# Products on a tile of ones at the head of a fused attention and soft-MoE kernel, and VectorE's fills of memory moved in front

## The chip, the cores and the metric

The kernel runs on 1 core of one Trainium2 chip. The metric is the device time of one execution in microseconds (us). TensorE (PE) multiplies, VectorE (DVE), ScalarE (ACT) and GpSimd (POOL) do the rest; GpSimd's queue issues all loads (with a conversion from float32 to bf16 on the way), SyncE's queue the stores.

## What is computed

Two stages follow each other. Attention with a softmax that has one extra term in its sum, over q, k and v of shape (8, 12, 448, 64), so 96 heads:

```python
scores = scale * np.matmul(q, k.transpose(0, 1, 3, 2))
m = np.max(scores, axis=-1, keepdims=True)
e = np.exp(scores - m)
attn = e / (np.sum(e, axis=-1, keepdims=True) + np.exp(-m) + 1e-09)
attn_out = np.matmul(attn, v)
```

Its result, turned into x of shape (3584, 768), goes through a mixture of experts with soft slots (8 experts, 4 slots each, hidden size 1024):

```python
logits = x @ phi
d = softmax(logits, over the 3584 rows);  c = softmax(logits, over the 32 slots)
slot_input = d.T @ x
slot_out[e] = np.maximum(slot_input[e] @ w1[e], 0.0) @ w2[e]
out = c @ slot_out
```

## The kernel before, in words

The order on every engine is the order of the program text; there is no scheduler. The 96 heads are worked in 48 pairs n, three pairs to a group g of loads. For a pair the steps are:

- `load(g, nm)` (L154 to L168): loads q, k or v of a group from GpSimd's queue. For group 0, q and k come pair by pair (`pl`), so six small loads, then v in two, then q and k of group 1. `make_identity` runs on GpSimd after the first two loads.
- `T(n)` (L214, product L224): 28 transposes of 64x64 on TensorE, two at a time on the two halves of the rows, into one buffer of `psA`; a copy to `R` follows, on ScalarE (L227) or VectorE (L229).
- `A(n, i)` (L237): scores with the queries on the partitions, for quarter i of the 448 queries. Quarters 0 to 2 are two products of 448 columns (L246), one for each head of the pair, each in a buffer of `psA`, and a row maximum on VectorE for each (L250); quarter 3 is two products in one buffer (L256) and one maximum (L259). So a pair costs VectorE seven maxima. `As(c)` runs the next c quarters in the list of all. Later in the kernel `A1` (L261, product L268, maximum L270) does the same for one head.
- `W1(g)`, `W2(g)`, `W3(g)`: GpSimd negates the maxima (L277), TensorE turns them (L297, and L298 with `ident2`), ScalarE takes them to `mT` (L303).
- `Bk(n, i)` (L313): scores with the keys on the partitions (L332, L335; later L354, L358 in `AB`), buffers of `psB`, and ScalarE's exponential into the five buffers of `e2`.
- `V(g)` (L372): GpSimd copies v into `vp`, whose columns of ones VectorE has written.
- `AV(n, i, qs)` (L381, product L393): the exponentials times v, in the one bank of `psV`. `N1` and `N2` divide, `PX` turns the result, and `P(b)` does logits and the sums over slots after each of the 8 batches.

`psA` has three buffers, so a product of `A` waits until the maximum three buffers back has been read. The experts follow after the last pair (`hidden`, `turn`, `slots`, `out_mm` at L793), and the stores.

At the start, ahead of the first pair, VectorE forms `ident2` and `identf` from `ident` (L181, L182), then fills memory: `halfm` (L190, L192), the two tiles `wm` (L194), the two tiles `vp` with their columns of ones (L196 to L199) and `ones` (L200, L201). After that come the first steps of the pipeline, written out by hand:

```python
T(0)
As(2)
T(1)
As(2)
W1(0)
V(0)
load(1, "v")
As(1)
T(2)
W2(0)
```

Then a loop over the pairs, of two half steps each, runs `As`, `Bk`, `T`, `AV` and the rest; its first five half steps run three quarters of `A` between `Bk`'s products and one at the end.

Of the kernel before, what the change touches and what calls it, by code (L numbers as in the profile page):

```python
# [8 lines left out]
F32 = mybir.dt.float32  # L9
# [15 lines left out]
HG = 6  # L25
NP = 3
W65 = 65
# [4 lines left out]
def kernel(  # L32
# [10 lines left out]
    nc = tc.nc  # L43
    B, H, S, D = q.shape
# [27 lines left out]
    ones = const.tile([128, 2], BF16, name="ones")  # L72
    sel = const.tile([128, HG], BF16, name="sel")
    phi_sb = const.tile([128, KC, NS], BF16, name="phi_sb")
    halfm = const.tile([128, 2], F32, name="halfm")
# [13 lines left out]
    part = lambda nm, o, z: R[:, at_[nm] + o:at_[nm] + o + z]  # L89
# [3 lines left out]
    vp = [part(f"vp{i}", 0, VPN).rearrange("p (h i d) -> p h i d", h=HG, i=4) for i in range(2)]  # L93
    wm = [part(f"wm{i}", 0, 512).rearrange("p (i c) -> p i c", i=4) for i in range(2)]
# [48 lines left out]
    with ExitStack() as at:  # L143
# [5 lines left out]
        psV = pool("psV", 1, space=PSUM)  # L149
# [4 lines left out]
        def load(g, nm, l0=0, l1=NP):  # L154


            b, h0 = g // 2, (g % 2) * HG
            src = {"q": q, "k": k, "v": v}[nm][b, h0:h0 + HG]
            if nm != "v":
                t = part(f"nq{g % 2}", "qk".index(nm) * NP * S, NP * S).rearrange("p (l x) -> p l x", l=NP)  # L160
                x = src.rearrange("(l h) (j t) d -> (h j) l (t d)", h=2, t=7)
                gdma(out=t[:, l0:l1, :], in_=x[:, l0:l1, :])
            else:
                t = part("nv", 0, NATV).rearrange("p (h t d) -> p h t d", h=HG, t=4)
                x = src.rearrange("h (p t) d -> p h t d", t=7)
                gdma(out=t[0:64], in_=x[:, :, 0:4, :])
                gdma(out=t[64:128], in_=x[:, :, 3:7, :])
            nat[nm, g] = t  # L168

        for pl in range(NP):  # L170
            load(0, "q", pl, pl + 1)
            load(0, "k", pl, pl + 1)
            if pl == 0:
                make_identity(nc, ident)
# [9 lines left out]
        for base in (0, 64):  # L184
# [2 lines left out]
                out=sel[base:base + 64], in_=sel[base:base + 64], fill=1.0,  # L187
                compare_op=ALU.not_equal, base=0,
                pattern=[[-1, HG]], channel_multiplier=1)
        nc.vector.memset(halfm, 0.0)  # L190
        for hl in range(2):
            nc.vector.memset(halfm[64 - 64 * hl:128 - 64 * hl, hl:hl + 1], 1.0)  # L192
        for t in wm:
            nc.vector.memset(t, 0.0)  # L194
        for t in vp:
            nc.vector.memset(t, 0.0)  # L196
            nc.vector.memset(t[:, :, 0:3, D:W65], 1.0)
            nc.vector.memset(t[0:64, 0:HG:2, 3, D:W65], 1.0)
            nc.vector.memset(t[64:128, 1:HG:2, 3, D:W65], 1.0)  # L199
        nc.vector.memset(ones, 1.0)  # L200
        nc.vector.memset(ones[64:128, 1:2], 0.0)  # L201
        gdma(out=phi_sb, in_=moe_phi.rearrange("(j p) s -> p j s", p=128))

        mx, ngm, ec, mT, eT, av, us = {}, {}, {}, {}, {}, {}, {}
# [9 lines left out]
        def T(n):  # L214
            g, pl = divmod(n, NP)
            ps = psA.tile([128, 2, S], BF16, tag="a", name="ps_t")
            for a in range(2):
                src = nat["qk"[a], g]
                for tok in range(7):
                    for hl in range(2):  # L220

                        c = kcol(hl, tok) if a else (2 * tok if tok < 4 else 2 * tok - 7) * 64
                        r = slice(64 * hl, 64 * hl + 64)
                        nc.tensor.transpose(ps[r, a, c:c + 64], src[r, pl, tok * D:(tok + 1) * D], ident[r, r])  # L224
            t = qk_t[n % NQK]
            if n < 6 or pl == 0:
                nc.scalar.copy(t, ps)  # L227
            else:
                nc.vector.tensor_copy(t, ps)  # L229
            qkT[n] = t  # L230
# [6 lines left out]
        def A(n, i):  # L237
            g, pl = mg(n), n % NP
            if pl == mpl(g)[0] and i == 0:
                mx[g] = psm.tile([128, 21], F32, tag="mx", name="mx")  # L240
            t = qkT[n]
            if i < 3:
                pss = [psA.tile([128, 512], F32, tag="a", name="ps_a") for _ in range(2)]
                for hl in range(2):
                    r = slice(64 * hl, 64 * hl + 64)
                    nc.tensor.matmul(pss[hl][:, 0:S], t[r, 0, i * 128:(i + 1) * 128], t[r, 1, :],  # L246
                                     start=True, stop=True)
                for hl in range(2):
                    c = HG * i + 2 * pl + hl
                    nc.vector.reduce_max(mx[g][:, c:c + 1], pss[hl][:, 0:S], axis=AX.X)  # L250
            else:
                ps = psA.tile([128, 512], F32, tag="a", name="ps_a")

                for hl in range(2):
                    r = slice(64 * hl, 64 * hl + 64)
                    nc.tensor.matmul(ps[64 - 64 * hl:128 - 64 * hl, 0:S], t[r, 0, 384:448], t[r, 1, :],  # L256
                                     start=True, stop=True)
                c = 3 * HG + pl
                nc.vector.reduce_max(mx[g][:, c:c + 1], ps[:, 0:S], axis=AX.X)  # L259
# [13 lines left out]
        def W1(g):  # L273
            w, m = wm[g % 2], mx[g]
            l0, l1 = mpl(g)
            nm = psm.tile([128, 21], BF16, tag="ngm", name="ngm")
            neg = lambda o, s: nc.gpsimd.tensor_scalar(o, s, -1.0, None, op0=ALU.mult)  # L277
            cols = lambda t: t[:, 0:3 * HG].rearrange("p (i c) -> p i c", i=3)[:, :, 2 * l0:2 * l1]
            o = w[:, 0:3, :].rearrange("p i (d c) -> p i d c", d=2)[:, :, :, 2 * l0:2 * l1]
            neg(o, cols(m).unsqueeze(2).to_broadcast([128, 3, 2, 2 * (l1 - l0)]))  # L280
            for hl in range(2):
                r = slice(64 - 64 * hl, 128 - 64 * hl)
                o = w[r, 3, :].rearrange("p (d c) -> p d c", d=2)[:, :, 2 * l0 + hl:2 * l1:2]
                neg(o, m[r, 3 * HG + l0:3 * HG + l1].unsqueeze(1).to_broadcast([64, 2, l1 - l0]))
            if l1 - l0 == NP:
                neg(nm, m)
            else:
                nc.gpsimd.memset(nm, 0.0)
                neg(cols(nm), cols(m))
                neg(nm[:, 3 * HG + l0:3 * HG + l1], m[:, 3 * HG + l0:3 * HG + l1])  # L290
            ngm[g] = nm
# [313 lines left out]
        def As(c):  # L605
            for _ in range(min(c, len(runs))):
                A(*runs.pop(0))


        T(0)  # L610
        As(2)
        T(1)
        As(2)
        W1(0)
        V(0)
        load(1, "v")
# [102 lines left out]
        n = NPAIR - 1  # L719
# [107 lines left out]
        for half in range(2):  # L827
            ps = psA.tile([128, 512], F32, tag="a", name="ps_cs")
            r = slice(64 * half, 64 * half + 64)
            for b2 in range(2):  # L830
                nc.tensor.matmul(ps[64 * b2:64 * b2 + 64, 0:2 * B], identf[r, r], crec[r, b2::2, :],
                                 start=True, stop=True)
# [54 lines left out]
```

## Time and profile before

| | us |
|---|---|
| median of 3 runs | 310.43 (310.2 to 311.73) |
| profiled execution, its own time | 310.7 |
| its span, first to last instruction | 308.9 |

| engine | busy us | share of the span |
|---|---|---|
| PE | 275.6 | 89% |
| DVE | 257.2 | 83% |
| ACT | 249.3 | 81% |
| POOL | 202.7 | 66% |

The page cuts the span into 40 slices of 7.7 us and gives busy tenths of each engine. A line of the timeline gives the start in us, the busy time, engine, line of the kernel, operation, output and input, shapes, the number of instructions merged, and in brackets the idle time of the engine before it with what ended it. The chain of waits follows the work that ended last back from the end. "PEld" is TensorE's load of weights, beside its products. Durations of products are modelled from their start and include the way through the array, so two that follow each other overlap.

### The profile page before, as it was taken

To read this page: it belongs to the slowest core of one execution; us is meant where nothing else is said; L and a number is where in the kernel's file an instruction comes from. 1 tells how busy PE (TensorE), PEld (TensorE's weight loads), DVE (VectorE), ACT (ScalarE), POOL (GpSimd) and SP (SyncE) were. 2 spreads that over 40 slices of the span, in tenths; PEclk is the share of its full clock that TensorE was granted. 3 is DMA by queue.
4 is the path that set the end of the run, shared out by engine and by line. 5 is a ranking of instruction groups with operands and counts; after the bars stand their busy time and mean duration, and the time that the engine had idled before them with its cause. 6 is when DMAs were issued, how large, how long until landed. Compare 5 with 4: busy or idle time off the path is not lost.

```text
span 308.9 us, 12205 instructions
## 1 busy us (share of the span) xinstructions
PE 275.6 (89%) x5067; PEld 159.0 (51%) x5068; DVE 257.2 (83%) x607; ACT 249.3 (81%) x549; POOL 202.7 (66%) x403
## 2 busy tenths in 40 slices
PE   2899999999999999999999999999999899994810
PEld 1434456565666656665566566656665556451200
DVE  4778999999999999999999999999999566536930
ACT  2357599999999999999999999999999997236810
POOL 8682769788788878896889788879584863000000
PEclk9999999999999999999999999999999999999555
DMA  6999499999999999999999999999971999937997
GB/s 88 149 128 202 64 205 150 198 182 205 163 196 157 210 169 198 155 203 149 149 164 186 177 186 169 196 177 203 166 110 17 144 126 204 337 128 260 415 439 312
DMA packets 49350, 57.44 MB, mean 186 GB/s; under 512 B 2832, under 2 KB 41488, under 8 KB 48912
## 3 DMA queue, kind: packets, MB, share of 16 engines
q0 software_dynamic: 45536, 42.52, 90.1%
q1 hardware_dynamic: 3760, 14.16, 11.5%
q8 instruction: 39, 0.64, 0.8%
q14 instruction: 15, 0.12, 0.1%
HBM read 88.18 MB, written 14.16 MB: 331 GB/s over the span
## 4 chain that ended last, share of the span: by engine, by line
PE 50%; DVE 30%; ACT 7%; issue 4%; POOL 4%; DMA 1%; DVEq 0%; POOLq 0%
DVE mx L270 15%; PE ps_av L393 11%; PE ps_a L268 6%; PE ps_t L224 6%; PE ps_b L354 5%; PE ps_b L358 4%; DVE mx L250 3%; DVE mx L259 3%; PE ps_b L332 3%; PE ps_a L246 2%; DVE W L801 2%; DVE R L229 2%; PE ps_x L445 2%; ACT R L227 2%; PE ps_so L764 2%
## 5 line engine op out<-in xcount | busy, mean ns | idle before, releaser
L270 DVE TENSOR_REDUCE mx<-ps_a 128x1 f32<-128x448 f32 x248 | 136.6, 613 | 5.3 <-PE ps_a L268 5.1
L360 ACT ACTIVATE R<-ps_b 128x448 bf16<-128x448 f32 x272 | 131.0, 573 | 1.1 <-PE ps_b L358 0.8
L268 PE MATMUL ps_a<-R 64*128 64x448 bf16 x248 | 80.5, 352 | 1.8 <-DVE mx L270 1.8
L354 PE MATMUL ps_b<-R 64*128 64x448 bf16 x272 | 73.9, 353 | 0.9
L358 PE MATMUL ps_b<-mT,sel 64*128 64x448 bf16 x272 | 70.6, 350 | 0.0
L393 PEld LDWEIGHTS <-R 128*128 128x128 bf16 (+1 forms) x1536 | 50.5, 101 | 30.5 <-issue 26.4
L393 PE MATMUL ps_av<-R 128*128 128x65 bf16 (+1 forms) x1536 | 64.9, 196 | 0.1
L419 POOL TENSOR_TENSOR R<-ubuf,rec 128x384 bf16<-128x384 f32 x44 | 36.3, 825 | 37.9 <-DVE rec L415 23.4
L224 PEld LDWEIGHTS <-R 64*64 64x64 bf16 x1344 | 31.1, 113 | 19.2 <-issue 7.8
L338 ACT ACTIVATE R<-ps_b 128x448 bf16<-128x448 f32 x64 | 36.0, 579 | 5.9 <-PE ps_b L335 5.9
L224 PE MATMUL ps_t<-ident,R 64*64 64x64 bf16 x1344 | 32.0, 198 | 5.9 <-DMA R<-in_q_dram 4.3
L451 ACT CAST R<-ps_x 128x512 bf16<-128x512 f32 x47 | 28.1, 598 | 5.7 <-PE ps_x L445 5.7
L259 DVE TENSOR_REDUCE mx<-ps_a 128x1 f32<-128x448 f32 x48 | 29.6, 616 | 0.6 <-PE ps_a L256 0.3
L358 PEld LDWEIGHTS <-sel 64*128 64x128 bf16 x272 | 21.5, 94 | 14.9 <-issue 5.3
L268 PEld LDWEIGHTS <-R 64*128 64x128 bf16 x248 | 23.1, 94 | 9.8
L405 ACT COPY ubuf<-ps_av 128x455 f32<-128x455 f32 x44 | 25.2, 573 | 3.0 <-PE ps_av L393 2.8
L227 ACT COPY R<-ps_t 128x896 bf16<-128x896 bf16 x20 | 18.4, 922 | 11.3 <-PE ps_t L224 11.0
L250 DVE TENSOR_REDUCE mx<-ps_a 128x1 f32<-128x448 f32 x40 | 22.6, 618 | 4.3 <-PE ps_a L246 3.9
L332 PE MATMUL ps_b<-R 64*64 64x448 bf16 (+1 forms) x112 | 22.7, 386 | 0.0
L335 PE MATMUL ps_b<-mT,sel 64*64 64x448 bf16 (+1 forms) x112 | 21.5, 366 | 0.0
L424 POOL TENSOR_TENSOR R<-ubuf,rec 128x128 bf16<-128x128 f32 x44 | 17.5, 398 | 3.7
L354 PEld LDWEIGHTS <-R 64*128 64x128 bf16 x272 | 17.2, 94 | 4.7 <-issue 0.2
(132 smaller groups left out, 454.0 us busy)
## 6 DMA issues: line engine op xcount, KB each, us to landing
W<-in_moe_w_dram POOLq DMA_DIRECT2D x22, 768.0 KB, 9.5
R<-in_v_dram POOLq DMA_DIRECT2D x32, 192.0 KB, 4.6
out_dram<-W SPq DMA_DIRECT2D x2, 2688.0 KB, 10.3
R<-in_q_dram POOLq DMA_DIRECT2D x15, 336.0 KB, 7.4
R<-in_k_dram POOLq DMA_DIRECT2D x15, 336.0 KB, 8.5
wd<-in_moe_w_dram POOLq DMA_DIRECT2D x8, 384.0 KB, 10.0
R<-wd SPq DMA_DIRECT2D x8, 384.0 KB, 8.6
R<-in_moe_w_dram POOLq DMA_DIRECT2D x2, 768.0 KB, 8.3
```

The lines of the kernel that those rows point to most:

```text
L224: nc.tensor.transpose(ps[r, a, c:c + 64], src[r, pl, tok * D:(tok + 1) * D], ident[r, r])
L250: nc.vector.reduce_max(mx[g][:, c:c + 1], pss[hl][:, 0:S], axis=AX.X)
L259: nc.vector.reduce_max(mx[g][:, c:c + 1], ps[:, 0:S], axis=AX.X)
L268: nc.tensor.matmul(ps[:, 0:S], t[r, 0, i * 128:(i + 1) * 128], t[r, 1, :], start=True, stop=True)
L270: nc.vector.reduce_max(mx[g][:, c:c + 1], ps[:, 0:S], axis=AX.X)
L332: nc.tensor.matmul(outs[hl], t[rs[hl], 1, cols], t[rs[hl], 0, :], start=True, stop=False)
L338: nc.scalar.activation(e, p[:, 0:S], AF.Exp, scale=scale)
L354: nc.tensor.matmul(ps[hl][:, 0:S], t[rs[hl], 1, cols], t[rs[hl], 0, :], start=True, stop=False)
L358: nc.tensor.matmul(ps[hl][:, 0:S], sel[rs[hl], h:h + 1].to_broadcast([64, 128]), mT[mg(n)][rs[hl], :], start=False, stop=True)
L360: nc.scalar.activation(e[:, hl, :], ps[hl][:, 0:S], AF.Exp, scale=scale)
L393: nc.tensor.matmul(o, eT[n, i, hl][:, qc], vp[g % 2][:, 2 * pl + hl, i, 0:W65], start=(i == 0 and u == 0 and hl == 0), stop=(i == 3), skip ...
L419: eng.tensor_mul(x[:, 0:3, c:c + 128].rearrange("p i (h d) -> p i h d", h=2), u[:, 0:6, 0:D].rearrange("p (i h) d -> p i h d", h=2), rec[: ...
```

## The change

A view `warm_t` of the first 512 columns of `e2` is filled with ones by VectorE as its first instruction, followed by all its fills of `halfm`, `wm`, `vp` and `ones`. TensorE gets seven products of 512 columns on that tile, with 128x128 of it as weights, ahead of everything else; they write a tile of the `psV` pool that nothing reads. The loads, `make_identity`, `ident2`, `identf` and `sel` follow in the text. GpSimd's order of instructions is as before. Five more such products, of 448 columns, stand between the first steps: two after T(0), one inside the first `As(2)`, one inside the second and one after it.

```diff
-        for pl in range(NP):
-            load(0, "q", pl, pl + 1)
-            load(0, "k", pl, pl + 1)
-            if pl == 0:
-                make_identity(nc, ident)
-        load(0, "v")
-        load(1, "q")
-        load(1, "k")
-
-
-        for h in range(2):
-            nc.vector.tensor_add(ident2[:, 64 * h:64 * h + 64], ident[:, 0:64], ident[:, 64:128])
-        nc.vector.tensor_copy(identf, ident)
-        nc.gpsimd.memset(sel, 0.0)
...
+        warm_t = part("e2", 0, 512)
+        nc.vector.memset(warm_t, 1.0)
+        ps_w = psV.tile([128, 512], F32, tag="v", name="ps_warm")
+
+        def warm(n, cols=512):
+            for _ in range(n):
+                nc.tensor.matmul(ps_w[:, 0:cols], warm_t[:, 0:128], warm_t[:, 0:cols], start=True, stop=True)
+
         nc.vector.memset(halfm, 0.0)
...
         nc.vector.memset(ones, 1.0)
         nc.vector.memset(ones[64:128, 1:2], 0.0)
+        warm(7)
+        for pl in range(NP):
+            load(0, "q", pl, pl + 1)
+            load(0, "k", pl, pl + 1)
+            if pl == 0:
+                make_identity(nc, ident)
...
         T(0)
-        As(2)
+        warm(2, S)
+        As(1)
+        warm(1, S)
+        As(1)
         T(1)
-        As(2)
+        As(1)
+        warm(1, S)
+        As(1)
+        warm(1, S)
         W1(0)
         V(0)
```

More of the change, by code (lines that the diff above doesn't have):

```diff
@@ L168, in load @@
             nat[nm, g] = t
+        warm_t = part("e2", 0, 512)
[4 more added lines that the diff above has]
+                nc.tensor.matmul(ps_w[:, 0:cols], warm_t[:, 0:128], warm_t[:, 0:cols], start=True, stop=True)
+        nc.vector.memset(halfm, 0.0)
+        for hl in range(2):
+            nc.vector.memset(halfm[64 - 64 * hl:128 - 64 * hl, hl:hl + 1], 1.0)
+        for t in wm:
+            nc.vector.memset(t, 0.0)
+        for t in vp:
+            nc.vector.memset(t, 0.0)
+            nc.vector.memset(t[:, :, 0:3, D:W65], 1.0)
+            nc.vector.memset(t[0:64, 0:HG:2, 3, D:W65], 1.0)
+            nc.vector.memset(t[64:128, 1:HG:2, 3, D:W65], 1.0)
+        nc.vector.memset(ones, 1.0)
+        nc.vector.memset(ones[64:128, 1:2], 0.0)
+        warm(7)
         for pl in range(NP):
@@ L189 @@
                 pattern=[[-1, HG]], channel_multiplier=1)
[L190 to L201, printed above, removed]
         gdma(out=phi_sb, in_=moe_phi.rearrange("(j p) s -> p j s", p=128))
```

## The prediction, made before the changed kernel ran

> **What bounds it.** I read the page first, then the timeline of the first 40 us, the chain of waits there, and a table of stretches cut at one repeated event.
>
> ```profile
> PE 275.6 (89%) x5067; PEld 159.0 (51%) x5068; DVE 257.2 (83%) x607; ACT 249.3 (81%) x549; POOL 202.7 (66%) x403
> DVE  4778999999999999999999999999999566536930
> PEclk9999999999999999999999999999999999999555
> ```
>
> VectorE is at 9 tenths from the fifth slice on, but has holes in the first four (31 us). The clock row says "full" there; the durations disagree. From the timeline:
>
> ```profile
> 8.27 0.95 PE L224 MATMUL ps_t<-ident,R 64*64 64x64 bf16 x28
> 22.97 0.82 PE L393 MATMUL ps_av<-R 128*128 128x65 bf16 x12
> 23.73 0.36 PE L246 MATMUL ps_a<-R 64*128 64x448 bf16 x2
> 31.41 0.63 PE L224 MATMUL ps_t<-ident,R 64*64 64x64 bf16 x28 [0.18 <-DVE mx L259]
> 31.97 0.54 PE L393 MATMUL ps_av<-R 128*128 128x65 bf16 x12
> ```
>
> The same 28 transposes take 0.95 us early and 0.63 later, the same 12 products 0.82 and 0.54; an L246 pair takes 0.55 to 0.58 before 23 us and 0.36 at 23.73. So TensorE runs at about half clock until some 23.5 us; the clock row simply has no record before that. What this costs is read from VectorE's waits:
>
> ```profile
> 7.06 2.22 DVE L250 TENSOR_REDUCE mx<-ps_a 128x1 f32<-128x448 f32 x4
> 9.74 1.16 DVE L250 TENSOR_REDUCE mx<-ps_a 128x1 f32<-128x448 f32 x2 [0.47 <-PE ps_a L246]
> 11.04 0.62 DVE L259 TENSOR_REDUCE mx<-ps_a 128x1 f32<-128x448 f32 x1
> 13.68 2.22 DVE L250 TENSOR_REDUCE mx<-ps_a 128x1 f32<-128x448 f32 x4 [0.95 <-PE ps_a L246]
> ```
>
> and from stretches cut where the maxima of A(1,1), A(2,1), A(3,1) and so on begin: equal work, seven maxima each.
>
> ```profile
> 13.68:18.79 5.11, 4.94 (x44) 1.80 (x44) 4.00 (x7) 3.02 (x8) 5.05 (x9) 1.00 0.79 85
> 18.79:24.12 5.33, 5.01 (x59) 2.30 (x58) 4.09 (x7) 2.80 (x5) 4.04 (x11) 1.00 1.16 156
> 24.12:28.60 4.48, 4.18 (x69) 2.14 (x69) 3.81 (x7) 3.67 (x9) 1.07 (x3) 1.00 1.32 205
> 28.60:32.83 4.23, 3.57 (x56) 1.65 (x56) 4.09 (x9) 2.51 (x5) 0.00 (x0) 1.00 0.90 138
> 32.83:37.31 4.48, 3.96 (x66) 2.04 (x67) 4.34 (x8) 2.37 (x6) 4.33 (x7) 1.00 0.26 25
> ```
>
> Columns: length, then busy time of PE, PEld, DVE, ACT, POOL. Two steps at half clock last 5.11 and 5.33 us with TensorE nearly full (4.94, 5.01); three at full clock last 4.48, 4.23 and 4.48, mean 4.40, with VectorE nearly full. The start is bound by TensorE at half clock, what follows by VectorE and TensorE together.
>
> **The change, part by part.** The sum is against the profiled execution: span 308.9, time 310.7, so 1.8 lie outside; it is 0.27 above the median of 310.43.
>
> *Fills moved.* VectorE's fills (L190 to L201) ran from 3.56 to 7.03; its first maximum began at 7.06, but that maximum's product ended only at 6.46 + 0.55 = 7.01. Moved in front, where VectorE sat idle 3.1 us for `ident`, fills plus the 0.6 of `ident2` and `identf` (L181, L182) end near 0.75 + 0.5 + 3.5 + 0.6 = 5.35. Alone that gains 0.03; with a faster product the maximum is free to start earlier. `ident2` and `identf` are not read before L298 at 12.89, so their delay costs nothing. SP's queue has nothing here, POOL's order is unchanged: the same issues, from 1.25 on.
>
> *Seven products in front.* The new fill is 512 bf16 elements of value 1; L196 takes 0.72 for 792 elements, so about 0.5. VectorE can start at 0.75, as ScalarE does (its table load), so the products can start near 1.3. A 448-column step at half clock is 0.37 (chain of waits, L332); 512 columns are 0.42, seven 2.94, ending near 4.25. The first transpose waits for q until 4.35, so q's transfer hides them with 0.1 to spare. Bounds: 0 if that holds, 0.3 late if the fill starts late; I take 0. No row shows an all-ones fill this early; L196 is nearest.
>
> *Five products in the waits*, 0.37 each at half clock, 0.19 at full. Two after T(0): TensorE idles from 5.5 to 6.46 for ScalarE's copy; hidden. One inside As(2): the next product's maximum queues behind two others until 8.17; hidden. One after A(0,2): the hole before 10.42 is 0.6; hidden. The last delays A(1,0) from 10.93 to 11.17 at half clock, up to 0.24; at full clock nothing. I charge 0.1. They write the bank that AV(0) takes at 22.97, long after.
>
> *What full clock brings*, if it comes by about 6.5 us:
> - First maximum: its product takes 0.36, not 0.55: 0.20.
> - A(0,2): T(1) starts with a freed bank near 8.07 and takes 0.63 plus 0.36, to 9.06; VectorE is busy until 9.08. The hole of 0.47 closes.
> - A(0,3): product 0.37, not 0.58; the hole of 0.14 before 11.04 closes.
> - A(1,1): hole 0.95. Before it POOL turns the maxima (L277) until 12.34, which no clock shortens; L297 starts 0.2 earlier, its step shrinks by 0.2, the product by 0.19: 0.6.
> - The two steps of 5.11 and 5.33 become 4.40: 0.71 + 0.93 = 1.64.
>
> Sum 0.20 + 0.47 + 0.14 + 0.6 + 1.64 = 3.05, less 0.1: about 2.9. The ceiling is all VectorE idle time from 7.06 to 24.13, 17.07 - 13.16 = 3.9. Next late is VectorE's own row of maxima. The gain should carry to the end: in the table of waits TensorE waits for a transfer once only, the 4.3 at the start, and POOL issues later loads in program order, earlier with the rest.
>
> *Does the clock come?* Unbroken TensorE work from 14.36 to 18.77 (4.41 us in the chain) did not raise it; from 20.03 to about 23.7 did. Most products there use half the array, paired. Seven full-array products back to back are denser than either, though only 2.94 long; then come 0.9 of transposes and 0.75 of products. I take it that it rises between 4.5 and 6.6. It must also stay: 28.60 to 32.83 held full clock with PE busy 3.57 of 4.23, and the new start is at least about as busy.
> The Trainium skill, TensorE: Matmul & The Clock Gate, Part 1, asks for about 3.4 us of sustained work in a free-running window; by it the seven alone fall short in some phases and the two after T(0) must help. Its Part 4 says that transposes do not count as busy; by that rule the gap grows and the forecast leans to the first rival's 310.7. No run here shows a start with dense products.
>
> *The tail.* At the end the clock halves near 286. Products of L793 on the chain after 289 sum to 3.1 us. A shifted start can move that drop against the work: at most 1.5 gained, 0.5 lost; I take 0.
>
> 310.7 - 2.9 = 307.8, and I forecast 307.8 for the median as well.
>
> **The rivals.**
> *The clock stays low or falls back.* For it: 4.41 us of unbroken work did not raise it. Against: the density above. Then the five products cost up to 0.24, and the time is 310.5 to 310.9, say 310.7; a rise one step late (near 13.7) keeps the 1.64 alone, about 309.1. Chance 0.15.
> *The gain is given back later*, by POOL or a transfer that becomes the bound. For it: the software queue's packets fill 90.1% of the span. Against: the single transfer wait, and q of group 2, issued at 16.25 with a median of 7.4 to landing, is used at 31.4. Time 309 to 310.4. Chance 0.07.
> *Slower: VectorE's fills hold back POOL's issues.* Fills now run beside the first q and k issues and the making of `ident`. If each held POOL until they end near 4.8, q would land up to 3.55 later than 4.30, TensorE would idle between the seven products and T(0), lose the clock, and the time be 310.7 + 3.5 = 314.2. It decides from a delay of 2.9 if the clock stays, of 1.6 (0.5%, about what a measurement here can tell) if it is lost. Against:
>
> ```profile
> 1.95 0.55 POOL L162 DMA_DIRECT2D R<-in_k_dram  x1
> 3.59 0.54 POOL L162 DMA_DIRECT2D R<-in_k_dram  x1
> 4.63 0.56 POOL L162 DMA_DIRECT2D R<-in_k_dram  x1
> ```
>
> The second and third lay beside fills, the first beside an idle VectorE: no difference. Chance 0.08.
> The Trainium skill, SBUF - State Buffer, SBUF: two separate sides, describes this trap (VectorE locking POOL out while it writes descriptors), which would give the 314.2; its Who interferes with whom exempts instructions with at most one input in SBUF, as fills are, which gives 307.8. The rows side with the exemption.
>
> **How the numbers follow.** Forecast 0.70, rivals 0.15, 0.07, 0.08. Faster by over 0.5% means below 308.9: the forecast. Within: both gentle rivals, 0.22. Slower: 0.08. The range goes down to 306.5 (the ceiling of 3.9, 306.8, and some of the tail) and up to 310.6, into the first rival; outside lie the slow rival and a few hundredths on each side.
>
> **What would show it.** Right: transposes of T(1) at 0.63, not 0.95; L246 pairs near 0.36 from 6.5 us; the hole of 0.47 gone, that of 0.95 down to about 0.35; steps near 4.4 from the first; the maxima of A(3,1) about 2.9 earlier than 24.12, and the last store earlier by the same. Wrong: half-clock durations past 10 us; a first transpose later than 4.5; q issues longer than 0.7; or A(3,1) early but the end not.

## The result, and the profile after

The changed kernel took 308.6 us (median of 11 runs, 307.47 to 310.6) against 311.27 for the kernel before (median of 11, 309.84 to 312.0): ratio 0.9922, 95% interval 0.99 to 0.9943, or 2.4 us. Twice more, beside the experiments, the ratio was 0.9881 (0.9839 to 0.9923) and 0.9938 (0.99 to 0.9977). The forecast was 307.8, against a median of 310.43 that stands at 311.27 now that there are more runs.

The first profile of the changed kernel is of an execution of 310.6 us, the slowest of its runs, with a span of 308.8 against 308.9 before. It is the more instructive for that: it shows the gain made and then lost. In this kernel's numbering L224 of before is L233, L246 is L255, L250 is L259, L539 is L548. From the page, busy tenths and clock:

```profile
PE   7878999999999999989999999999999899994810
DVE  5969999999999999979999999999999566536930
PEclk9979999999999999999999999999999999999555
```

VectorE fills its second and fourth slice as before it did only from the fifth, but has new holes in slices 3 and 18, and the clock row shows a 7 in slice 3, where before it had no record at all. The start, from the timeline:

```profile
0.93 0.48 DVE L171 MEMSET R<- 128x512 bf16 x1 [0.93 <-PEq L886]
1.47 3.17 PE L176 MATMUL ps_warm<-R 128*128 128x512 bf16 x7 [1.47 <-DVE halfm L178]
4.57 0.85 PE L233 MATMUL ps_t<-ident,R 64*64 64x64 bf16 x28
5.46 0.91 ACT L236 COPY R<-ps_t 128x896 bf16<-128x896 bf16 x1 [3.43 <-PE ps_t L233]
6.82 3.32 DVE L259 TENSOR_REDUCE mx<-ps_a 128x1 f32<-128x448 f32 x6 [1.54 <-PE ps_a L255]
8.03 0.63 PE L233 MATMUL ps_t<-ident,R 64*64 64x64 bf16 x28 [0.19 <-DVE mx L259]
12.02 2.22 DVE L259 TENSOR_REDUCE mx<-ps_a 128x1 f32<-128x448 f32 x4 [0.20 <-PE ps_a L255]
```

T(1) takes 0.63 us, which before was first so for T(4), at 26.9 us; six maxima follow each other without a hole where there was one of 0.47; the hole before A(1,1) is 0.20, not 0.95, and A(1,1) starts at 12.02, not 13.68. In the trace's record of the clock, full speed begins at 5.15 us (23.64 before). Then:

```profile
14.82 0.41 PE L233 MATMUL ps_t<-ident,R 64*64 64x64 bf16 x14 [0.18 <-DVE mx L268]
16.66 0.41 PE L233 MATMUL ps_t<-ident,R 64*64 64x64 bf16 x14 [1.43 <-DMA R<-in_k_dram]
17.40 2.22 DVE L259 TENSOR_REDUCE mx<-ps_a 128x1 f32<-128x448 f32 x4 [1.57 <-PE ps_a L255]
20.20 0.95 PE L233 MATMUL ps_t<-ident,R 64*64 64x64 bf16 x28
25.22 0.63 PE L233 MATMUL ps_t<-ident,R 64*64 64x64 bf16 x28 [0.18 <-DVE mx L268]
```

T(3) does its 14 transposes of q, then stands 1.43 us for k of group 1. Soon after, the clock falls, and T(4) at 20.20 takes 0.95 again. The stretches between 5.2 and 30 us (columns as above; the sixth number after the length is the granted clock):

```profile
5.20:18.80 13.60, 10.01 (x145) 4.33 (x141) 10.29 (x20) 6.20 (x11) 12.03 (x26) 1.00 1.16 146
18.81:22.20 3.39, 3.39 (x51) 1.90 (x50) 2.50 (x5) 2.36 (x4) 3.05 (x9) 0.50 1.17 171
22.30:30.00 7.70, 6.75 (x103) 3.13 (x103) 6.92 (x13) 5.43 (x12) 1.24 (x3) 1.00 1.30 202
```

So the lead over the kernel before was 2.7 us at A(2,0), 14.7 us in, and 1.7 at A(3,1) (22.42 against 24.12). It stayed 1.7 to 1.8 up to 131 us, and was lost there:

```profile
131.48 0.25 PE L233 MATMUL ps_t<-ident,R 64*64 64x64 bf16 x5 [0.34 <-issue]
138.50 0.18 PE L548 MATMUL ps_s<-cd,R 128*128 128x32 bf16 x1 [1.28 <-issue]
```

TensorE stops after 23 of 28 transposes, and again after 23 of 28 products, for 0.34 and 1.28 us, with no wait that the profile shows. From 139 us on the lead is 0.1. The profile of the kernel before has no such stop.

### The profile page after: what moved, and what is told of

The parts are those of the page before. It is cut to its first block, busy times and chain, and to the rows that moved or that the text cites. A ratio compares the mean times of both kernels' runs of the same rounds, so it can differ in the third digit from the quotient of the medians.

```text
span 308.8 us, 12231 instructions
## 1 busy us (share of the span) xinstructions
PE 276.0 (89%) x5079; PEld 159.0 (51%) x5080; DVE 257.2 (83%) x608; ACT 249.4 (81%) x549; POOL 203.4 (66%) x403
## 4 chain that ended last, share of the span: by engine, by line
PE 49%; DVE 27%; ACT 7%; POOL 5%; issue 4%; DMA 3%; DVEq 0%; POOLq 0%
DVE mx L279 14%; PE ps_av L402 11%; PE ps_a L277 6%; PE ps_b L363 5%; PE ps_t L233 5%; PE ps_b L367 4%; DMA R<-in_k_dram 3%; DVE mx L259 3%; PE ps_b L341 3%; DVE mx L268 2%; PE ps_x L454 2%; PE ps_so L779 2%; PE ps_o L808 2%; PE ps_h L763 2%; DVE R L238 2%
## 5 line engine op out<-in xcount | busy, mean ns | idle before, releaser
L233 PEld LDWEIGHTS <-R 64*64 64x64 bf16 x1344 | 30.3, 110 | 16.5 <-issue 7.1
L233 PE MATMUL ps_t<-ident,R 64*64 64x64 bf16 x1344 | 31.0, 195 | 3.6 <-DMA R<-in_k_dram 1.4
L259 DVE TENSOR_REDUCE mx<-ps_a 128x1 f32<-128x448 f32 x40 | 22.5, 618 | 5.3 <-PE ps_a L255 5.1
L341 PE MATMUL ps_b<-R 64*64 64x448 bf16 (+1 forms) x112 | 21.8, 374 | 0.0
L344 PE MATMUL ps_b<-mT,sel 64*64 64x448 bf16 (+1 forms) x112 | 20.7, 353 | 0.0
```

What stands on the lines that cost most here:

```text
L341: nc.tensor.matmul(outs[hl], t[rs[hl], 1, cols], t[rs[hl], 0, :], start=True, stop=False)
```

## The experiments

The theory now: the seven products raise the clock, the five hold it, and two things can take a part back, k's transfer and TensorE's stops. Rivals: the moved fills carry the gain; the five alone do; any busy TensorE does, whatever share of the array works; the stops belong to the change. In each list below, "lead" is against the profiled execution of the kernel before, at the first maximum of A(3,1) (24.12 us there) and at the last store's issue.

**again**: the changed kernel, unchanged.

> The changed kernel once more, for a second profile. In its first profile the lead over the kernel before was 2.7 us at 14.7 us, 1.7 from 22 us on, and 0.1 from 139 us on, after TensorE had stood 0.3 us at 131.1 and 1.3 us at 137.2 with nothing to wait for. Theory 'chance': those two stops are not of the change, so this profile keeps a lead of 1.7 to 2.7 us to the end and its span is 306 to 307.2. Rival 'given back': the shifted program meets them each time, and the lead is gone at 139 us again, span 308.5 or more. Timed, either way, 0.990 to 0.994 of the kernel before.

Median 307.4 (6 runs); before 311.39 (29 runs); ratio 0.9881 (0.9839 to 0.9923). Clock up at 5.42 us, T(3) waits for k (landed at 17.02), clock down at 19.08 for 3.4 us; lead 1.4 at A(3,1) and 1.2 at the last store. No stop at 131 to 139. The ratio is better than the 0.990 to 0.994 expected. The lead kept to the end is a little under what "chance" expected; the span of 307.4 lies between the two forecasts. The stops are not part of each execution. The wait for k is:

```profile
17.06 0.41 PE L233 MATMUL ps_t<-ident,R 64*64 64x64 bf16 x14 [1.69 <-DMA R<-in_k_dram]
```

**fills_only**: fills in front, no products.

```diff
-        warm_t = part("e2", 0, 512)
-        nc.vector.memset(warm_t, 1.0)
...
-        warm(7)
...
-        warm(2, S)
...
```

> VectorE's fills in front, none of the twelve products. Theory 'clock': the transposes of T(1) still take 0.95 us, the first maximum starts within 0.1 us of 7.06, the ratio is 0.999 to 1.001. Rival 'order': the moved fills carry the gain, and the ratio is 0.990 to 0.994 as for the whole change.

Median 310.89 (12 runs), ratio 0.9982 (0.9945 to 1.0018). The first maximum starts at 7.03, not 7.06, T(1) takes 0.96, clock up at 23.41 (23.64 before); the lead at A(4,1) is 0.1. The moved fills alone bring nothing that the runs can show; the interval does not hold the 0.9922 of the whole change.

**seven_only** and **seven_look**: the same kernel twice, without the five.

```diff
-        warm(2, S)
-        As(1)
-        warm(1, S)
-        As(1)
+        As(2)
...
-        warm(1, S)
-        As(1)
-        warm(1, S)
+        As(1)
```

> The seven products in front, none of the five in the waits. Theory 'the seven raise the clock, the five only guard it': in most runs the whole gain, ratio 0.990 to 0.995; in the profile full clock by about 7 us. Rival 'the five are needed': the clock stays at half or falls back before 14 us, ratio 0.997 to 1.000.

> The seven without the five once more, one look. In the first the clock rose at 23.6 us only. Theory 'the seven can raise it, in some positions of a clock of its own, and the five hold it': full clock by 5.5 us and back to half before 15 us, or as in the first look. Rival 'the seven never raise it': half clock to 17 us or later again.

seven_only: median 310.92 (12 runs), ratio 0.9986 (0.9954 to 1.0019), no gain to be seen; its profile had half clock to 23.64 us. seven_look is one execution, of 310.48 us, and its profile caught the clock in the act (transposes of T(0), T(1), T(2), then stretches of the same run):

```profile
4.57 0.95 PE L233 MATMUL ps_t<-ident,R 64*64 64x64 bf16 x28
8.14 0.63 PE L233 MATMUL ps_t<-ident,R 64*64 64x64 bf16 x28 [0.19 <-DVE mx L259]
11.07 0.96 PE L233 MATMUL ps_t<-ident,R 64*64 64x64 bf16 x28 [0.23 <-DVE mx L268]
```

```profile
6.00:9.40 3.40, 2.02 (x34) 0.83 (x34) 2.47 (x5) 1.07 (x2) 3.18 (x7) 1.00 1.12 146
9.50:23.00 13.50, 12.53 (x137) 5.65 (x136) 10.53 (x19) 6.66 (x14) 10.69 (x26) 0.50 1.18 154
```

Half, full, half: up at 6.0 us, down at 9.4, up at 23.1. The seven can raise the clock, and without the five it fell back 3.4 us later, though TensorE was busy 2.02 of 3.40 us. The timed runs say how often. Time ahead of the first record counts as full clock in a run's mean granted clock (0.964 in the profile of the kernel before, despite its start), so a rise without a fall leaves no mark in it, but a fall does: it is 0.941 in seven_look, and 0.938 to 0.945 in 7 of the 12 runs of seven_only, against 0.961 to 0.964 in the other five, of which one is the profile with half clock to 23.64. So the seven alone raised the clock in at least 7 of 12 runs, and there it fell back. In fills_only, five_only and half_rows no run is under 0.958.

**five_only**: without the seven.

```diff
-        warm(7)
```

> The five products in the waits, not the seven in front. Theory 'the seven raise the clock': full clock comes somewhat earlier than in the kernel before, between 10 and 17 us, for the waits are denser: a third to two thirds of the gain, ratio 0.994 to 0.998. Rival 'the five do it': T(1) at 0.63 us and ratio 0.990 to 0.994. Rival 'density in the waits does nothing': half clock past 17 us, ratio 0.999 to 1.001.

Median 310.19 (12 runs), ratio 0.9965 (0.9935 to 0.9996). Clock up at 18.07 us; lead 1.3 at A(3,1). The ratio is the theory's; the clock, in the one profile, rose later than its 10 to 17 us, as in the last rival. The rise came 5.6 us earlier than before (23.64), so the five can bring it forward; what that is worth, some 1.1 us by the ratio, has an interval of 0.1 to 2.0.

**half_rows**: all twelve on 64 rows of the array.

```diff
-                nc.tensor.matmul(ps_w[:, 0:cols], warm_t[:, 0:128], warm_t[:, 0:cols], start=True, stop=True)
+                nc.tensor.matmul(ps_w[:, 0:cols], warm_t[0:64, 0:128], warm_t[0:64, 0:cols], start=True, stop=True)
```

> The twelve products with 64 rows of the tile instead of 128: the same number of columns and the same time each, half of the array at work. Theory 'the share of the array counts': the clock does not rise in front, the products only fill time, ratio 0.996 to 1.000, half clock past 13 us. Rival 'only time counts': as the change, full clock by about 7 us in most runs, ratio 0.988 to 0.994.

Median 310.93 (12 runs), ratio 0.999 (0.9959 to 1.0021). The seven take the same time, but the clock stays at half to 23.45:

```profile
1.47 3.17 PE L176 MATMUL ps_warm<-R 64*128 64x512 bf16 x7 [1.47 <-DVE halfm L178]
8.32 0.95 PE L233 MATMUL ps_t<-ident,R 64*64 64x64 bf16 x28
11.84 0.96 PE L233 MATMUL ps_t<-ident,R 64*64 64x64 bf16 x28
```

Time alone does not count, the share of the array does. The profile alone would not show it, for in seven_only's profile the full array did not raise the clock either; the 12 runs do, with an interval that does not hold 0.9922 and no granted clock under 0.959.

**split_next**: the first third of group 1's q and k ahead of the rest.

```diff
-        load(1, "q")
-        load(1, "k")
+        load(1, "q", 0, 1)
+        load(1, "k", 0, 1)
+        load(1, "q", 1, NP)
+        load(1, "k", 1, NP)
```

> The changed kernel with the first third of the next group's q and k (all that T(3) reads) loaded ahead of their other two thirds, so two more issues on GpSimd's queue. In both profiles of the change T(3) stood 1.4 to 1.6 us for k of group 1, and the clock then fell for 3.4 us at about 19 us. Theory 'the transfer takes back a part': k's third lands before 15 us, the wait is gone, the clock stays up past 19 us, and the maximum of A(3,1), at 22.4 in the first profile of the change, starts near 20.8; 1 to 1.7 us faster than the changed kernel, ratio to before 0.983 to 0.989. Rival 'another wait takes its place': v or GpSimd's later start of W1 holds, and the ratio is that of the change, 0.989 to 0.993.

Median 308.16 (6 runs), ratio 0.9891 (0.9855 to 0.9926). k's third landed at 12.65, T(3) did not wait (1.43 and 1.69 us in the two profiles of the change), A(1,1) to A(2,1) took 3.77 us (5.38 in the first profile of the change). But in this profile the clock had already fallen, from 9.42 to 12.83:

```profile
6.10:9.40 3.30, 2.58 (x36) 1.00 (x35) 2.48 (x5) 0.97 (x2) 3.23 (x7) 1.00 1.17 143
9.50:12.80 3.30, 3.30 (x39) 1.58 (x38) 2.52 (x5) 0.57 (x2) 2.56 (x9) 0.50 1.25 183
```

Even so the lead was 2.9 at A(3,1) and 2.7 at the last store, with a span of 306.2. A(3,1) began at 21.20, not near 20.8. The transfer's part is confirmed in the profile; the ratio is the rival's, so in the medians the kernel is not told from the change.

**hold**: four more products ahead of T(3).

```diff
+                if hs == 0:
+                    warm(4, S)
                 if hs < 5:
                     T(hs + 3)
```

> The changed kernel with four more products of 448 columns ahead of T(3), in the time in which TensorE waits for k of group 1. The transfer is not moved. Theory 'the wait costs twice, by itself and by the clock': the wait of 1.4 to 1.6 us stays, but full clock holds past 19 us, and A(3,1) starts 0.5 to 0.9 us earlier than 22.4; ratio to the kernel before 0.986 to 0.990. Rival 'the fall of the clock does not matter there': the same ratio as the change, 0.989 to 0.993.

Median 308.01 (6 runs), ratio 0.9886 (0.9849 to 0.9924). The clock rose at 4.47 and held to 284; lead 3.3 at A(3,1), then two stops at 85 and 98 us, and 1.5 at the last store. As a test of the wait it is inconclusive: this time k landed at 15.19, and T(3) began at 15.63, after the four products. Whether it would have waited without them is not shown.

**dense** and **again2**: split_next with four more products, beside the change on the same chip. The diff leaves out the load order. (The text on dense says that T(3) waited for k in hold; that was misread: it stood behind the four products.)

```diff
         T(0)
         warm(2, S)
         As(1)
-        warm(1, S)
+        warm(2, S)
         As(1)
         T(1)
         As(1)
-        warm(1, S)
+        warm(2, S)
...
+                if hs == 0:
+                    warm(2, S)
                 if hs < 5:
                     T(hs + 3)
```

> The load order of split_next, and four more products: two instead of one inside each As(2), two ahead of T(3). In split_next the clock fell at 9.4 us with the waits of 6.0 to 9.4 filled by one product, and the lead was 2.7 us; in hold it never fell, but T(3) still waited 0.9 us for k, and the lead was 3.3. Theory 'clock and transfer are two separate losses': neither comes, the lead over the kernel before at A(6,1) is 3.5 to 4.3 us, and the ratio to the kernel before is 0.984 to 0.988. Rival 'the start is by then bound by VectorE': the lead is 3.3 or less, ratio 0.988 to 0.991, as hold and split_next.

> The changed kernel beside dense on the same chip. Ratio to the kernel before 0.988 to 0.994; dense is 0.5 to 1.5 us faster by its median if the lead of its start counts, within 0.4 us if TensorE's stops at random places cover it.

dense: median 308.23 (8 runs, 307.4 to 308.39), ratio 0.9907 (0.9873 to 0.9941). Clock up at 5.64, held to 282; lead 3.6 at A(3,1), 3.5 at A(6,1), 2.2 at the last store, after one stop of 1.1 at 188 us. The lead is the theory's at its lower end, the ratio the rival's. again2: median 308.5 (9 runs, 307.39 to 311.65), ratio 0.9938 (0.99 to 0.9977), and the best start of all, lead 4.0 at A(3,1): this time k landed at 15.14, and T(3) hardly waited:

```profile
14.70 0.89 PE L233 MATMUL ps_t<-ident,R 64*64 64x64 bf16 x28 [0.18 <-DVE mx L268]
15.92 2.22 DVE L259 TENSOR_REDUCE mx<-ps_a 128x1 f32<-128x448 f32 x4 [0.21 <-PE ps_a L255]
18.72 0.63 PE L233 MATMUL ps_t<-ident,R 64*64 64x64 bf16 x28 [0.18 <-DVE mx L268]
```

By 177 us half of that lead was gone, most of it in these two stops, and 1.8 was left at the last store:

```profile
129.61 0.25 PE L233 MATMUL ps_t<-ident,R 64*64 64x64 bf16 x5 [0.54 <-issue]
176.12 0.43 PE L402 MATMUL ps_av<-R 128*128 128x65 bf16 x9 [0.98 <-issue]
```

dense is 0.3 us faster by its median, within the 0.4 of "stops cover it". Its runs lie closer together, but with 8 against 9 runs and the same fastest time (307.4), no version here is shown to beat the change. The two slowest runs of again2, 310.36 and 311.65 us, have a mean granted clock of 0.948 and 0.939 (0.958 to 0.963 in its other seven): there the clock fell back in the changed kernel too, 0.939 being as low as in seven_look. No run of dense is under 0.96. With two runs against none, that the extra products prevent the fall is not shown.

## Why the prediction was right, and where it was not

- **Half clock at the start, and its price.** Right. The starts with full clock and no late transfer bear the mechanism out; the sizes were too small. In again2 A(1,1) started 1.78 earlier (1.41 in the sum: 0.20 + 0.47 + 0.14 + 0.6), and the two next steps took 4.02 and 4.23 us, not 4.40: 2.2 instead of 1.64. Together 3.97 instead of 3.05. The most mis-sized term is the step: three later ones were averaged, though the first step of the start has no products of AV yet and the second has 12, as the later step of 4.23. The rest is mostly the first maximum, 0.36 earlier and not 0.20, and the hole before A(1,1), which shrank by 0.75 and not 0.6.
- **The seven hidden behind q.** Off by 0.2 without effect. VectorE began its fill at 0.93, not 0.75, so the products began at 1.47, and T(0) at 4.57 instead of 4.35. T(0)'s second half waits for k (4.77) anyway, and ScalarE's copy began at 5.46 (5.50 before).
- **The five for nothing.** Right at full clock: no maximum waits behind them. At half clock they cost more than the 0.24: in five_only A(1,0) began at 11.95, 0.37 later than before.
- **"I take it that it rises between 4.5 and 6.6."** Right in the three profiles of the change (5.15, 5.42, 4.86). **"It must also stay"** failed in two of them, once T(3) had stood for k: the comparison with the stretch from 28.60 to 32.83 looked at the average of the start, not at its emptiest 3.4 us.
- **"The gain should carry to the end", because TensorE waits for a transfer once only.** This step failed. That nothing waited for k of group 1 before said only that T(3) came later: k landed at 15.25 and T(3) began at 17.31. A gain of 2.7 us is more than those 2.06 of slack, and k landed later still (16.62 and 17.02) in two profiles of the change. In place of the lead of 2.9 at A(3,1) and at the last store these two showed 1.7 and 1.4 there, and 0.1 and 1.2 at the end; TensorE's stops, a term that the sum did not have, took 1.6 from the first.
- **Why the time still came out.** In part by luck. The start was worth more than forecast (4.0 us in again2, not 2.9), and less of it was kept: k's late transfer, the fall of the clock and the stops took parts of it back, so 0.1, 1.2 and 1.8 us were left at the last store of the three profiles. The median gain of 2.4 lies near the 2.9 because these errors oppose each other. How often a timed run meets each of them is not known.
- **What would show it.** T(1) at 0.63, the hole of 0.47 gone and that of 0.95 down to 0.20 came as named. So did three signs of being wrong: half clock past 10 us (T(4) in the first profile), a first transpose later than 4.5 (4.57, without effect) and an early A(3,1) without an early end (the first profile). They point at the two steps above, the clock that must stay and the gain that should carry.
- **The rivals.** The slow one did not happen: POOL's first issues took 0.71, 0.55, 0.55 and 0.54 us beside the fills, q landed at 4.23 (4.30 before). That agrees with what the Trainium skill, SBUF - State Buffer, Who interferes with whom, says of VectorE's instructions with at most one input in SBUF, outside the modes that use both ports: they do not contend with GpSimd. The first rival, a clock that falls back, came true in part: for 3.4 us at a time in two profiles, and by the granted clock for longer in two of again2's runs. The second, a gain given back later, came true in the first profile, by k's transfer and by the stops, which no rival named.

## What to carry to other kernels

Read TensorE's clock from the durations of equal products, early against late: a clock row without records looks like full speed. Dense products on the full array ahead of the first data raised it here in most executions, but the waits that follow had to be filled too, or it fell again. And before a start is made faster, compare when each early transfer lands with when it is first used: the absence of a wait is not slack.

## What the runs showed of the hardware that was not expected

**The clock follows the work in the array, in steps of 3.41 us.** In the trace's records of granted clock, the early stretches that end in another change last 3.41 or 13.65 us (four times 3.41). The Trainium skill, TensorE: Matmul & The Clock Gate, Part 1, gives such a free-running window, and these runs agree: with the seven in front an early rise came anywhere from 4.47 to 6.01 us. Taking for each 3.41 us that ended in a change the columns of all products at the clock they ran at, times the share of the array's rows and columns that they use, the early rises came after 0.61 to 0.91 (0.88 in the first profile of the change, 0.65 in seven_look, 0.70 in five_only) and none after 0.43 in half_rows, though TensorE streamed for 0.86 of that time; 0.61 to 0.63 also occurs without a rise, so no sharp limit is shown. In seven_only's profile the windows, counted back from its rise at 23.64, cut the seven in two, 0.50 and 0.49, and the clock stayed at half. The two products after T(0) would have added some 0.2 to the second window (an estimate, from 0.37 us each).

The Trainium skill has, in the same Part 1, the clock fall after an idle window; here that does not fit. It fell after 0.22 in seven_look and 0.32 in split_next, with TensorE busy 2.02 of 3.40 and 2.58 of 3.30 us, and stayed at 0.33 to 0.35 in hold and in again2. The measured falls decide.

**TensorE's stops end when a packet of instructions has come.** Counting its products and weight loads by their records, the 16 stops of over 0.2 us in all profiles come before number 1984, 2752, 3264, 4544, 4800, 6336 or 6848 (4544 and 4800 in the first profile of the change): all distances are multiples of 256. The queue of kind "instruction" moved 39 packets of 16 KB in each run, about one for each 256 of some 10,150 instructions. The packets' times in the traces tie the two together: each of the 16 stops ended 1.29 to 1.55 us after the end of the last such packet, and in no run did TensorE pass one of these places, which stand 256 instructions apart, sooner than 1.19 us after it (the first place comes before any packet). So the stops are read as waits for code: where the packet was late, TensorE stood. Why it is late in one execution and in time in the next stays open, and no experiment here tried to change it. The stops, up to 2 us in one profile, and the falls of the clock both add to the spread of the runs; how much of the spread each makes is not shown.
